# Output stage of a gated mix of a state-space layer and an MLP: when the states are loaded, and where two buffers lie

## The chip, the cores and the metric

The kernel runs on one core of a Trainium2 chip. A core has a matrix engine (TensorE, PE in the profile), three engines for elementwise work (VectorE or DVE, ScalarE or ACT, GpSimd or POOL) and SyncE (SP), which here only issues transfers. Transfers are issued on the queues of SP, ACT and POOL, and 16 DMA engines carry them out. Each engine works through its own queue in order and waits on semaphores for the others.

The metric is the device time of one execution in microseconds, as the median over runs.

## The reference, cut to what matters

The input `x` has 2048 tokens of 1024 features. A gate `g` per token mixes a diagonal complex state-space layer and an MLP with layer norm; everything is given and returned in bfloat16.

```python
def reference(A_x, A_Lambda_re, ..., gate_w):
    def _A_ref(x, ...):
        Lam_bar = jnp.exp(dt * Lam)
        Bu = jnp.einsum("bld,pd->blp", x + 0j, B_bar)
        for t in range(L):
            h = Lam_bar[None, :] * h + Bu[:, t, :]
            hs.append(h)
        hseq = jnp.stack(hs, 1)
        y = 2.0 * jnp.einsum("blp,dp->bld", hseq, Cmat).real + x * Dskip[None, None, :]
        return y
    def _B_ref(x, w1, b1, w2, b2):
        y = _layernorm(x, axis=-1)
        h = _gelu(jnp.einsum("bsd,df->bsf", y, w1) + b1)
        return jnp.einsum("bsf,fd->bsd", h, w2) + b2
    x = A_x
    g = _sigmoid((x * gate_w).sum(-1, keepdims=True))
    a = _A_ref(...)
    b = _B_ref(...)
    return g * a + (1 - g) * b
```

## The kernel before

**Stages.** The kernel first multiplies `x` by `B` and stores the result in device memory, runs the recurrence as scans on DVE beside the MLP's matmuls, and stores the states (`HS`, one tensor of 1 MB for each 256 tokens). The MLP is done in halves of its hidden features: `m` groups compute hidden values into the area HT, `b` groups multiply them by `W2`. What a `b` group yields is scaled by 1 - g (`GM1`) and stored in float32 in `ACS` in device memory; the second half of the features is added there by an accumulating store (`acs1.k` for token tile k of 128 tokens, line 1243, on the POOL queue). Last comes the **output stage**: eight output blocks `y0` to `y7` of 256 tokens, two token tiles each, in the order `YORD` (tokens 1024 to 2047 first), so that `y0` holds token tiles 8 and 9, `y1` 10 and 11, `y4` 0 and 1.

**One group on PE.** Each group of the MLP and each output block is a 2x2 block product in Winograd's form, with seven products in place of eight. They are the phases p1 to p7 of the class `SG`, each 8 (in `b` groups 7) matmuls of 128x128 by 128x512. For block x the order is p1(x), p7(x-1), p5(x), p6(x), p2(x), p3(x), p4(x-1). Around them:

- the sums `ys1` to `ys4` (`y_prep`, made on DVE from the states): ys1 feeds p5, ys2 feeds p6, ys4 feeds p3 and ys3 feeds p7;
- `seed` (line 1053, ACT) copies the bank of p1 into a second bank, on which p6, p7 and p4 go on adding;
- the snapshots `s5` (after p5) and `su` (after p6), written by ACT to the memory on chip (line 1045);
- DVE's `oa` (line 1331, adds a snapshot) and `o` (line 1333, evicts a bank into the output tile), and the store `out` on the ACT queue (line 1338).

**What is loaded** (`y_load`). For block yi: `hg` (line 1298), the states, 1 MB on the SP queue into the slot `H0[yi]`; for each of the two token tiles, ACT's `bb` (line 1307), which fills a float32 slot with the bias; `acl` (line 1309), a load on the POOL queue that adds the MLP's result from `ACS` to that slot; `yx` (line 1310), the tile of `x` on the SP queue; then DVE's `xd` (line 1311, x times D) and `xa` (line 1312, adds it to the slot). `y_load` is called for blocks 0 and 1 at the last `b` group, for 2 and 3 at block 0, and for x+3 at block x.

**Areas.** The memory on chip is one arena with areas laid by hand: HT (the hidden values, 28 KB in each partition), W2Q right behind it (seven quadrants and differences of `W2`, 7 KB each: B11 at 0, B21 at 7168, B22 at 14336, and so on), W1R, XN, SQ, AO (18 KB: four slots of 4 KB for the `b` groups' results on their way to `ACS`, and s5 in the last 2 KB), SSM (20 KB) and TABR. The output stage uses them again. Before the change its eight state slots are two in SSM and six in HT and the first part of W2Q; the sums of even blocks lie in SQ (running 1 KB into AO) and those of odd blocks in AO from 4096 on, `su` of odd blocks in AO from 12288 on. The last two `b` groups' results use slots 0 and 1 (tiles 4 and 5) and 2 and 3 (tiles 6 and 7).

**The order.** The program is a graph of tasks. Dependencies follow from reads and writes of pieces of 256 bytes of the arena, so that a writer waits for all that read the bytes before it. A planner with costs and priorities written into the kernel lays the tasks on the engines' queues once, when the program is built; on the chip each queue keeps that order, whatever the true times are. `hg`, `bb`, `acl`, `yx`, `xd` and `xa` have priority 52, behind all of the MLP's and the output stage's own work (10): the planner fits them in wherever a queue has nothing else ready. `extra` adds dependencies by hand; `pe_last` is a list that holds the task that was last laid on PE.

Of the kernel before, what the change touches and what calls it, by code (L numbers as in the profile page):

```python
# [35 lines left out]
def c_act(N, psum=True, ap_operands=0):  # L36
    return (0.15 if psum else 0.19) + 0.00083 * N + 0.09 * ap_operands


def c_tt16(N):  # L40
    return 0.07 + N / 1920.0


def c_dve(N):
    return 0.09 + N / 960.0
# [374 lines left out]
def build(nc, A_x, A_Lambda_re, A_Lambda_im, A_B_re, A_B_im, A_C_re, A_C_im, A_log_dt, A_Dskip,  # L420
          B_x, B_w1, B_b1, B_w2, B_b2, gate_w, out, stats=None):
# [22 lines left out]
    g = Graph()  # L444
    es = ExitStack()
    with es:
# [5 lines left out]
        def sem(name, dram=False):  # L452
            nsem[0] += 1
            return SemC(es.enter_context(nc.semaphore(name)), name, dram)
# [3 lines left out]
        HS = nc.dram_tensor("scr_h", (L // T, 128, 2 * PT * T), BF16, kind="Internal").ap()  # L458
# [18 lines left out]
        HT = AR.alloc(28672)  # L477
# [3 lines left out]
        SQ = AR.alloc(14336)  # L481
        AO = AR.alloc(18432)
        SSM = AR.alloc(20480)
# [20 lines left out]
        def bc(name):  # L504
            if name not in b_cst:
                b_cst[name] = B("cst." + name)
            return b_cst[name]
# [14 lines left out]
        def ssem(name, k, final=False):  # L522
            key = (name, k)
            if key not in slot_sems:
                slot_sems[key] = sem("d_%s%d" % (name, k), dram=final)
                if final:
                    final_sems.append(slot_sems[key])
            return slot_sems[key]
# [39 lines left out]
        def C(name, j=0, n=1):  # L568
            return V(CST, col[name] + j, [(1, n)])
# [19 lines left out]
        def bcast(ap, off, name):  # L589
# [11 lines left out]
              reads=[b_ones], writes=[b_ident], name="ident")  # L601
# [77 lines left out]
        for k in range(4):  # L679
# [5 lines left out]
              reads=[b_stg, b_ident], writes=[b_ps[bk0]], name="cst_T", extra=[g.tasks[-2]])  # L685
        stage_names = ["LRE", "LIM", "LDT", "DSK", "B2", "GW", "B1"]
        cst_cp = g.add("dve", 0.15, P0, lambda e: e.tensor_copy(V(CST, 0, [(1, NROW)]), V(PS16[bk0], 0, [(1, NROW)])),
              reads=[b_ps[bk0]], writes=[bc(n) for n in stage_names] + [b_ps[bk0]], name="cst_copy")
# [97 lines left out]
        for p0 in range(0, PT, 4):  # L786
# [4 lines left out]
                  reads=[e1i], writes=[vt], name="tab_s%d" % p0)  # L791
        for pt in range(PT):
# [7 lines left out]
                  reads=[pi, bc("E20I")], writes=[td0], name="e2t0_%d" % pt)  # L800
            g.add("dve", 0.3, PT2, lambda e, td1=td1, pr=pr, pt=pt: e.tensor_scalar(td1.ap, pr.ap, C("E20I", pt), None, ALU.mult),
                  reads=[pr, bc("E20I")], writes=[td1], name="e2t1_%d" % pt)
            g.add("dve", c_dve(T), PT2, lambda e, td0=td0, pr=pr, pt=pt, o2=o2: e.scalar_tensor_tensor(o2.ap, pr.ap, C("E20R", pt), td0.ap, ALU.mult, ALU.add),
                  reads=[pr, td0, bc("E20R")], writes=[o2], name="e2r_%d" % pt)
            g.add("dve", c_dve(T), PT2, lambda e, td1=td1, pi=pi, pt=pt, o3=o3: e.scalar_tensor_tensor(o3.ap, pi.ap, C("E20R", pt), td1.ap, ALU.mult, ALU.subtract),
                  reads=[pi, td1, bc("E20R")], writes=[o3], name="ne2i_%d" % pt)
# [3 lines left out]
        b_hs = [[B("hs%d_%d" % (p, h)) for h in range(L // T)] for p in range(PT // 4)]  # L810
# [107 lines left out]
        for pt in range(4, PT):  # L918
            for ri, ap in enumerate((A_B_re, A_B_im)):
                o = AR.v(RB + (pt * 2 + ri) * 2048, [(128, DT), (1, 128)])  # L920
# [6 lines left out]
        for half in range(2):  # L927
            for pt in range(4, PT):
# [4 lines left out]
              reads=[bc(z) for z in zs], writes=[bc("TZ")], name="tanh")  # L933
        g.add("dve", 0.1, (5.0, 0), lambda e: e.tensor_scalar(C("G", 0, NTT), C("TZ", 0, NTT), 0.5, 0.5, ALU.mult, ALU.add),
              reads=[bc("TZ")], writes=[bc("G")], name="G")
        g.add("dve", 0.1, (5.0, 0), lambda e: e.tensor_scalar(C("GM1", 0, NTT), C("TZ", 0, NTT), -0.5, 0.5, ALU.mult, ALU.add),
              reads=[bc("TZ")], writes=[bc("GM1")], name="GM1")
# [6 lines left out]
        PG = PT // 4  # L944
        NQ = L // T
        UE = 8 * T
# [68 lines left out]
        pe_last = []  # L1015
# [230 lines left out]
        nxt_ss = {}  # L1246


        H0 = [SSM + 8192 * i for i in range(2)] + [HT + 8192 * i for i in range(6)]
        YR = HT + 49152  # L1250
        AV = [TABR + 4096 * i for i in range(4)] + [YR + 4096 * i for i in range(4)]
        XV = [SSM + 16384, YR + 16384, YR + 18432]
        DB = SSM + 18432
        OV = [YR + 20480 + 2048 * i for i in range(4)]
        YS = [SQ + 7168, AO + 4096]
        YU = [SSM + 16384, AO + 12288]
        CQ = {"B11": 0, "B21": 1, "B22": 2, "T1": 3, "T2": 4, "T3": 5, "T4": 6, "B12": 6}
        YORD = (4, 5, 6, 7, 0, 1, 2, 3)

        def cq(nm, k=None, dt=None):  # L1260
            dt = dt or (FP16 if nm[0] == "T" else BF16)
            if k is None:
                return AR.v(W1R + CQ[nm] * 8192, [(1, 4096)], dt)
            return AR.v(W1R + CQ[nm] * 8192 + k * 1024, [(1, 512)], dt)
# [9 lines left out]
        def hk(yi, ri, t, k=None):  # L1274
            o = H0[yi] + (ri * T + t * 128) * 2
            if k is None:
                return AR.v(o, [(2 * T, PT), (1, 128)])
            return AR.v(o + k * 4 * T, [(1, 128)])

        def ysq(yi, i, k=None):  # L1280
            o = YS[yi % 2] + i * 2048
            if k is None:
                return AR.v(o, [(128, PT), (1, 128)], FP16)
            return AR.v(o + k * 256, [(1, 128)], FP16)
# [9 lines left out]
        def y_load(yi):  # L1294

            qb = YORD[yi]
            o = AR.v(H0[yi], [(1, 2 * UE)])
            g.dma((52.0, yi), lambda e: e.dma_start(out=o.ap, in_=HS[qb]), 2 * UE * 128 * 2, ssem("hg", yi), reads=[b_hs[pg][qb] for pg in range(PG)], writes=[o], name="hg%d" % yi)
            if yi == 0:
                g.dma((51.0, 0), lambda e: e.dma_start(out=v_db.ap, in_=bass.AP(A_Dskip.tensor, A_Dskip.offset, [[0, 128], [1, D]])), 128 * D * 2, sem("d_dskb"), writes=[v_db], name="dskb")  # L1300
            for t in range(2):
                n = 2 * yi + t
                k = 2 * qb + t
                av = AR.v(AV[n % 8], [(1, D)], F32)
                xi = 0 if n < 4 else 1 + n % 2
                xv = AR.v(XV[xi], [(1, D)])
                g.add("act", c_act(D, psum=False, ap_operands=1), (52.0, n), lambda e, av=av, k=k: e.activation(av.ap, v_b2.ap, AF.Copy, scale=C("GM1", k)),  # L1307
                      reads=[v_b2, bc("GM1")], writes=[av], name="bb%d" % k)
                g.dma((52.0, n), lambda e, av=av, k=k: e.dma_start(out=av.ap, in_=ACS[k], accum_op=ALU.add), 128 * D * 4, ssem("yac", n % 8), reads=[b_acs[k], av], writes=[av], name="acl%d" % k, q="pool").slack = 1.0  # L1309
                g.dma((52.0, n), lambda e, xv=xv, k=k: e.dma_start(out=xv.ap, in_=x2[k * 128:(k + 1) * 128, :]), 128 * D * 2, ssem("yx", xi), writes=[xv], name="yx%d" % k)  # L1310
                g.add("dve", c_tt16(D), (52.0, n), lambda e, xv=xv: e.tensor_tensor(xv.ap, xv.ap, v_db.ap, ALU.mult), reads=[xv, v_db], writes=[xv], name="xd%d" % k)
                g.add("dve", c_dve(D), (52.0, n, 1), lambda e, xv=xv, av=av, k=k: e.scalar_tensor_tensor(av.ap, xv.ap, C("G", k), av.ap, ALU.mult, ALU.add),
                      reads=[xv, av, bc("G")], writes=[av], name="xa%d" % k)

        def y_group(yi):
# [4 lines left out]
            mv = {nm: [cq(nm, k) for k in range(PT)] for nm in ("B11", "B21", "B22", "T1", "T2", "T3", "T4")}  # L1320
            su, s5 = AR.v(YU[yi % 2], [(1, 512)], F32), AR.v(AO + 16384, [(1, 512)], F32)
            done = {}
# [59 lines left out]
        for n, it in enumerate(flat):  # L1382
# [4 lines left out]
            if (kind, Fh, c, x) == ("b", 1, 0, 3):  # L1387
                y_load(0)
                y_load(1)
            if (kind, x) == ("y", 0):  # L1390
                for yi in range(2, 4):
                    y_load(yi)
# [72 lines left out]
def bass_gated_mix__ssm_conv_s5__mixer_channel_mlp__prompt_kernel(  # L1465
    nc, A_x, A_Lambda_re, A_Lambda_im, A_B_re, A_B_im, A_C_re, A_C_im, A_log_dt, A_Dskip,
    B_x, B_w1, B_b1, B_w2, B_b2, gate_w, out,
):
    build(nc, A_x, A_Lambda_re, A_Lambda_im, A_B_re, A_B_im, A_C_re, A_C_im, A_log_dt, A_Dskip,
          B_x, B_w1, B_b1, B_w2, B_b2, gate_w, out)  # L1470
# [28 lines left out]
```

## Time and profile before

| what | value |
|---|---|
| time, median of 6 runs | 584.19 us (582.49 to 585.09) |
| time of the profiled execution | 584.37 us |
| its span, first to last instruction | 582.6 us |
| mean granted clock of TensorE | 0.994 |
| PE busy / DVE busy / ACT busy / POOL busy | 96% / 82% / 47% / 13% |
| DMA | 134.76 MB, mean 231 GB/s |
| state loads `hg` after 440 us | 6 of 1024 KB, median 15.2 us from issue to landing |
| accumulating loads `acl` after 440 us | 12 of 512 KB, median 8.7 us |
| stores `acs` after 440 us | 7 of 512 KB, median 11.6 us |
| `x` tiles `yx` after 440 us | 13 of 256 KB, median 4.8 us |

The span is what the profiler sees between the first and the last instruction; the time of the same execution is 1.8 us longer. Busy shares are averages over stages with different limits, so they say only which engine can't have much room over the whole span. The granted clock is 1 where TensorE runs at full speed. The last four rows are from the output stage and its entry: between issue and landing a transfer may stand behind others in its queue, and shares the 16 DMA engines with the other queues.

### The profile page before, as it was taken

How to read it: one execution, taken by the hardware profiler on the slowest of the kernel's cores; microseconds unless marked ns; L12 is line 12 of the kernel's file. 1: busy time of each engine (PE TensorE's matmuls, PEld its weight loads, DVE VectorE, ACT ScalarE, POOL GpSimd, SP SyncE). 2: the span in 40 equal slices, each digit the busy share in tenths (PEclk: the TensorE clock that was granted, in tenths of full speed). 3: DMA queues.
4: the chain of work that ended last, by engine and by line, in shares of the span. 5: the costliest groups of instructions: out<-in, count | busy, mean ns of one | idle time of the engine just before them, and what ended most of it. 6: DMA issues, size and time to landing. Idle time of an engine off the chain costs nothing.

```text
span 582.6 us, 7345 instructions
## 1 busy us (share of the span) xinstructions
PE 557.2 (96%) x2608; PEld 254.1 (44%) x2657; DVE 479.0 (82%) x817; ACT 272.3 (47%) x433; POOL 75.3 (13%) x110
## 2 busy tenths in 40 slices
PE   5999999998999999999999999999999996899997
PEld 4544444443444444444444444444444442344442
DVE  3897749959999999999999999996457745699843
ACT  3935861456773236862346763248652431222210
POOL 0070161000100110011110102221001130111000
PEclk9999999999999999999999999999999997999999
DMA  8999949998599354667398799896998699897411
GB/s 273 262 259 371 354 92 316 251 334 326 177 335 287 112 217 173 203 217 283 130 335 292 241 273 268 152 189 230 298 262 153 134 287 300 239 211 180 126 52 54
DMA packets 124543, 134.76 MB, mean 231 GB/s; under 512 B 70482, under 2 KB 100178, under 8 KB 123482
## 3 DMA queue, kind: packets, MB, share of 16 engines
q1 hardware_dynamic: 99664, 70.81, 43.4%
q0 software_dynamic: 11232, 46.40, 28.9%
q10 hardware_dynamic: 13610, 17.08, 8.8%
q8 instruction: 21, 0.34, 0.2%
q14 instruction: 16, 0.13, 0.1%
HBM read 63.74 MB, written 54.80 MB: 203 GB/s over the span
## 4 chain that ended last, share of the span: by engine, by line
PE 72%; DVE 15%; DMA 7%; issue 3%; ACT 1%; SPq 1%; ACTq 0%; DVEq 0%; POOLq 0%
PE ps L1029 44%; PE ps L1027 16%; PE ps L825 11%; DMA scr_ac<-ar 5%; DVE ar L970 3%; DVE ar L984 3%; DVE ar L1081 3%; DVE ar L973 2%; DVE ar L1163 2%; DMA ar<-in_B_w_dram 2%; DVE ar L871 1%; DMA ar<-in_A_x_dram 1%; PE ps L666 1%; PE ps L650 0%; DVE ar L1333 0%
## 5 line engine op out<-in xcount | busy, mean ns | idle before, releaser
L1029 PE MATMUL ps<-ar 128*128 128x512 f16 (+1 forms) x1419 | 326.7, 380 | 6.9 <-ACT ar L1045 3.8
L1029 PEld LDWEIGHTS ps<-ar 128*128 128x128 f16 (+1 forms) x1440 | 140.7, 98 | 178.3 <-ACT ar L1045 4.7
L1027 PE MATMUL ps<-ar 128*128 128x512 f16 (+1 forms) x560 | 139.2, 383 | 7.5 <-DVE ar L1081 6.8
L1081 DVE TENSOR_TENSOR ar<-ar 128x896 f16<-128x896 bf16 (+8 forms) x176 | 118.6, 709 | 28.8 <-DMA scr_ac<-ar 9.7
L825 PE MATMUL ps<-ar 128*128 128x512 bf16 x500 | 110.4, 379 | 0.7 <-issue 0.2
L1027 PEld LDWEIGHTS ps<-ar 128*128 128x128 bf16 (+1 forms) x576 | 56.3, 98 | 76.9 <-DVE ar L1081 9.2
L984 DVE TENSOR_TENSOR_SCAN ar<-cst,init,ar 128x256 bf16<-128x256 f32 x128 | 86.9, 731 | 0.3
L970 DVE TENSOR_TENSOR ar<-ar 128x2048 bf16<-128x2048 bf16 x64 | 77.0, 1217 | 3.0 <-DMA ar<-scr_u 2.9
L825 PEld LDWEIGHTS ps<-ar 128*128 128x128 bf16 x512 | 49.7, 98 | 59.6 <-issue 0.4
L1045 ACT ACTIVATE ar<-ps 128x512 f32<-128x512 f32 x72 | 42.3, 593 | 47.2 <-PE ps L1027 28.5
L832 ACT ACTIVATE ar<-ps 128x512 bf16<-128x512 f32 x64 | 37.1, 596 | 48.1 <-PE ps L825 25.4
L1163 DVE TENSOR_TENSOR ar<-ps,ar 128x512 f32<-128x512 f32 x56 | 38.1, 680 | 11.7 <-PE ps L1029 11.5
L1165 ACT ACTIVATE ar<-ar,cst 128x512 bf16<-128x512 f32 x56 | 40.3, 720 | 14.7 <-DVE ar L1163 14.4
L1046 ACT ACTIVATE ar<-ps,cst 128x512 f32<-128x512 f32 x32 | 22.1, 689 | 53.4 <-PE ps L1027 33.7
L1159 ACT ACTIVATE ar<-ps,cst 128x512 bf16<-128x512 f32 x56 | 38.3, 687 | 17.9 <-PE ps L1029 17.5
L1053 ACT ACTIVATE ps<-ps 128x512 f32<-128x512 f32 x52 | 30.3, 583 | 33.7 <-PE ps L1027 26.7
L973 DVE TENSOR_TENSOR ar<-ar 128x1024 bf16<-128x1024 bf16 x64 | 42.0, 685 | 0.3
L1231 ACT ACTIVATE ar<-ps,cst 128x512 f32<-128x512 f32 x32 | 22.1, 689 | 41.7 <-PE ps L1029 41.7
L1333 DVE SCALAR_TENSOR_TENSOR ar<-ps,cst,ar 128x512 bf16<-128x512 f32 x32 | 23.8, 747 | 13.9 <-PE ps L1029 13.9
L1307 ACT ACTIVATE ar<-ar,cst 128x1024 f32<-128x1024 bf16 x16 | 18.3, 1146 | 28.7 <-DVE ar L1333 27.1
L1234 DVE SCALAR_TENSOR_TENSOR ar<-ps,cst,ar 128x512 f32<-128x512 f32 x32 | 23.7, 739 | 6.5 <-PE ps L1029 6.3
L1309 POOL DMA_DIRECT2D ar<-scr_ac x16 | 14.0, 878 | 93.2 <-ACT ar L1307 55.0
(98 smaller groups left out, 224.0 us busy)
## 6 DMA issues: line engine op xcount, KB each, us to landing
scr_ac<-ar POOLq DMA_DIRECT2D x32, 512.0 KB, 5.5
scr_w<-ar POOLq DMA_DIRECT2D x14, 896.0 KB, 6.1
ar<-scr_w SPq DMA_DIRECT2D x14, 896.0 KB, 6.3
ar<-in_A_x_dram SPq DMA_DIRECT2D x32, 256.0 KB, 4.9
scr_u<-ar ACTq DMA_DIRECT2D x32, 256.0 KB, 5.7
ar<-scr_u SPq DMA_DIRECT2D x16, 512.0 KB, 8.0
scr_h<-ar POOLq DMA_DIRECT2D x16, 512.0 KB, 5.7
ar<-scr_ac POOLq DMA_DIRECT2D x16, 512.0 KB, 8.7
```

What stands on the lines that cost most here:

```text
L825: ins = e.matmul(V(PS[bk], 0, [(1, CH)]), ws[dt].ap, xs[dt].ap, start=(dt == 0), stop=(dt == DT - 1))
L832: g.add("act", c_act(CH), pr, lambda e, ev=ev, bk=bk: e.activation(ev.ap, V(PS[bk], 0, [(T, 2), (1, T)]), AF.Copy), reads=[b_ps[bk]], writ ...
L970: g.add("dve", c_tt16(UE), pri(i), lambda e: e.tensor_tensor(o.ap, a.ap, tbl.ap, ALU.mult), reads=[a, tbl], writes=[o], name=nm + tag)
L973: g.add("dve", c_tt16(UE // 2), pri(i), lambda e: e.tensor_tensor(o.ap, a.ap, b.ap, op), reads=[a, b], writes=[o], name=nm + tag)
L984: lambda e, pt=pt, ri=ri, vin=vin, go=go: e.tensor_tensor_scan(go.ap, Cb("R", pt, T), vin.ap, V(INIT, pt * 2 + ri, [(1, 1)]), ALU.mult, AL ...
L1027: ins = e.matmul(V(PS[bk], 0, [(1, n)]), st[i].ap, mv[i].ap, start=(i == 0), stop=(i == K - 1))
L1029: ins = e.matmul(V(PS[bk], 0, [(1, n)]), st[i].ap, mv[i].ap, start=False, stop=(i == K - 1), skip_group_check=True)
L1045: return e.activation(o.ap, V(PS[bk], 0, [(1, 512)]), AF.Copy)
L1081: g.add("dve", c_tt16(n), (10.0, q), lambda e: e.tensor_tensor(o.ap, a.ap, b.ap, op), reads=[a, b], writes=[o], name=nm).slack = slack
L1159: g.add("act", c_act(512, ap_operands=1), (10.0, q + 1), lambda e: e.activation(o.ap, V(PS[bk], 0, [(1, 512)]), AF.Gelu_apprx_tanh, bias=C ...
L1163: g.add("dve", c_dve(512), (10.0, q - 2), lambda e: e.tensor_tensor(sv.ap, V(PS[bk], 0, [(1, 512)]), sv.ap, ALU.add), reads=[b_ps[bk], sv] ...
L1165: g.add("act", c_act(512, psum=False, ap_operands=1), (10.0, q + 3), lambda e: e.activation(o.ap, sv.ap, AF.Gelu_apprx_tanh, bias=C("B1", ...
```

## The change

The state slots become a ring of six: blocks 6 and 7 use the two slots in SSM again, after blocks 0 and 1. The sums of odd blocks (`YS[1]`) move from AO to the place that the slot of block 6 had, in the quadrants B11 and B21 of W2Q, and `su` of odd blocks (`YU[1]`) to the start of the former slot of block 7, in B21. The state loads of blocks 4 to 7 get a dependency on the task that was last laid on PE when `y_load` is called for them, which is p4 of the block x-1 where the call is made at block x: p4 of blocks 0, 1, 2 and 3 for the loads of blocks 4, 5, 6 and 7.

```diff
-        H0 = [SSM + 8192 * i for i in range(2)] + [HT + 8192 * i for i in range(6)]
+        H0 = [SSM, SSM + 8192] + [HT + 8192 * i for i in range(4)] + [SSM, SSM + 8192]
         YR = HT + 49152
...
-        YS = [SQ + 7168, AO + 4096]
-        YU = [SSM + 16384, AO + 12288]
+        YS = [SQ + 7168, HT + 32768]
+        YU = [SSM + 16384, HT + 40960]
...
-            g.dma((52.0, yi), lambda e: e.dma_start(out=o.ap, in_=HS[qb]), 2 * UE * 128 * 2, ssem("hg", yi), reads=[b_hs[pg][qb] for pg in range(PG)], writes=[o], name="hg%d" % yi)
+            g.dma((52.0, yi), lambda e: e.dma_start(out=o.ap, in_=HS[qb]), 2 * UE * 128 * 2, ssem("hg", yi), reads=[b_hs[pg][qb] for pg in range(PG)], writes=[o], name="hg%d" % yi,
+                  extra=pe_last if yi > 3 else ())
```

The planner lays the queues anew. In the built program PE's order is the same. On DVE the sums of block 1 stand earlier, among the last `b` group's work; `xa13`, `xa12`, `xa15` and the following `xd` and `xa` take other places among the evictions, and `xa12` stands ahead of `o9.1`. On ACT, `seed` of block 1 comes before its neighbour `bb0`, and `seed` of block 2 comes after `out9` and `bb1`, where it stood before `out9`. On SP the state loads are spread: behind load 3 come `yx15`, `yx14`, `yx1`, load 4, `yx0`, load 5, `yx2`, `yx3`, load 6, `yx4`, `yx5`, load 7, `yx6`, `yx7`; before, loads 2, 6 and 7 stood together, and 3, 4 and 5. POOL's order is the same.

## Prediction

> **What bounds the kernel now.** I read the page first. TensorE (PE) is busy 96% of the span and makes up 72% of the chain that ended last, so only time in which PE stands still, or runs slowly, can be won. In the chain one link is no engine at all:
>
> ```profile
> PE 72%; DVE 15%; DMA 7%; issue 3%; ACT 1%; SPq 1%; ACTq 0%; DVEq 0%; POOLq 0%
> PE ps L1029 44%; PE ps L1027 16%; PE ps L825 11%; DMA scr_ac<-ar 5%; DVE ar L970 3%; DVE ar L984 3%; DVE ar L1081 3%; DVE ar L973 2%; DVE ar L1163 2%; DMA ar<-in_B_w_dram 2%; DVE ar L871 1%; DMA ar<-in_A_x_dram 1%; PE ps L666 1%; PE ps L650 0%; DVE ar L1333 0%
> ```
>
> Second, the chain in order of time (start, length, what) says where that link lies: at the entry to the output stage, one store of the MLP result takes 26.87 us, and behind it PE runs without a break until the last phase.
>
> ```profile
> 475.66 26.87 DMA scr_ac<-ar
> 507.33 7.08 PE ps L1029 x32
> 514.46 1.67 PE ps L1027 x7
> 516.14 1.73 PE ps L1029 x8
> ```
>
> Third, the waits of PE from 230 us to the end (total, times, longest). All but the 0.8 (the tail, which stays) and 0.8 of the 5.9 lie in 480 to 508 us:
>
> ```profile
> PE ps L1027 <- DVE ar L1081: 5.9, 3, 5.1
> PE ps L1029 <- ACT ar L1045: 1.8, 1, 1.8
> PE ps L1029 <- DVE ar L1333: 0.8, 1, 0.8
> PE ps L1029 <- ACT ps L1053: 0.5, 1, 0.5
> ```
>
> Fourth, the timeline of that stretch (start, length, then idle time and what ended it). The sums of output block 1 on VectorE (DVE) wait for the stores of the MLP staging they are written over: first ys3_1, then, at 487.36, ys1_1, which PE waits for. Then ScalarE (ACT) can't write the snapshot su_1 before the last store lands, and PE waits again:
>
> ```profile
> 483.67 0.69 DVE L1081 TENSOR_TENSOR ar<-ar 128x1024 f16<-128x1024 bf16 x1 [5.08 <-DMA scr_ac<-ar]
> ...
> 487.36 1.42 DVE L1081 TENSOR_TENSOR ar<-ar 128x1024 f16<-128x1024 bf16 x2 [1.14 <-DMA scr_ac<-ar]
> ...
> 488.11 3.60 PE L1027 MATMUL ps<-ar 128*128 128x512 f16 x8 [5.13 <-DVE ar L1081]
> ...
> 491.50 8.15 PE L1029 MATMUL ps<-ar 128*128 128x512 f16 x32
> ...
> 502.56 0.60 ACT L1045 ACTIVATE ar<-ps 128x512 f32<-128x512 f32 x1 [10.16 <-DMA scr_ac<-ar]
> ...
> 503.21 1.90 PE L1029 MATMUL ps<-ar 128*128 128x512 f16 x8 [1.84 <-ACT ar L1045]
> ```
>
> Fifth, three stretches of it (start:end, length, busy time of PE, PE's weight loads, DVE, ACT, POOL; the last three numbers are the granted clock, the DMA share and GB/s). After the 5.1 us pause the clock is at half, and the DMA engines are full:
>
> ```profile
> 483.00:486.00 3.00, 0.00 (x0) 0.00 (x0) 2.33 (x4) 0.54 (x1) 0.00 (x0) 1.00 1.05 274
> 486.00:488.00 2.00, 0.00 (x0) 0.00 (x0) 0.86 (x2) 1.09 (x2) 0.86 (x1) 0.71 1.06 326
> 488.00:490.00 2.00, 1.89 (x5) 0.73 (x6) 1.97 (x5) 0.00 (x0) 0.00 (x0) 0.50 1.06 311
> ```
>
> **What the waits cost.** Idle: 5.13 + 1.84 + 0.49 = 7.5 us. Slow clock: 8 matmuls from 488.11 to 491.50 took 3.39 against 1.73 in the chain, and the next 32, to 499.70, took 8.20 against 6.91: 1.66 + 1.29 = 2.95. Together 10.4. Check: from block 0's first phase (469.43) to 507.33 PE has 127 matmuls of 0.216 (6.91 / 32), 27.4 us; it took 37.9, so 10.5 were lost.
>
> **Part 1, the buffers.** YS[1] (the sums of odd blocks) and YU[1] (their su) leave AO for the area of W2's quadrants B11 and B21. Their new owners are PE's phases p1 and p2 of the last MLP group; p2 ends at about 464.8 (five phases fill 461.66 to 469.4). In the built program ys1_1, ys3_1 and ys2_1 stand behind DVE's work that ended at 464.4, 0.6 each, before the eviction of p3 (466.42 now, 467.2 at most then; its bank is wanted at 483.0). So both waits for stores go: 10.4 us. ys4_0 still overlaps AO's first KB and waits for the store acs1.4 (landed 470.6), but is due at 477.6. Nothing is added on PE, whose order is the same.
>
> **Part 2, the state loads.** Loads 4 to 7 (1 MB each) now wait for the last phase (p4) of blocks 0 to 3, and 6 and 7 reuse SSM. This takes 4.2 MB out of 465 to 502 us. It matters through the queues: loads 6 and 7 were issued at 464.9 and 466.4, and the x tiles 12 and 13 behind them on SP landed only at 482.9 and 486.1. Meanwhile the Pool queue's transfers (512 KB each) landed at 470.6, 475.7, 480.5, 483.6, 487.3, 492.9 (accumulating load acl12), 498.0, 502.5: 3.2 to 5.5 apart, where two stores with nothing beside them landed 2.96 apart.
>
> What is late next? The new DVE order has xa12 (adds x·D to the loaded sum; needs acl12) **ahead of** the eviction o9.1 and all that follows, so acl12 decides. Six Pool transfers follow the one that lands at 467.3. At 2.96 each: 485.0; at today's pace: 492.9. With only load 3 and two x tiles beside them I take 3.15 each, the gap seen beside x tiles alone (480.5 to 483.6): 486. From there, by the spacing in the timeline (1.2 an xa, 0.66 an eviction or oa, 0.6 a sum or xd): xa12 to 487.2; then thirteen instructions to o9.0, one xa, six evictions or oa, six sums or xd, 1.2 + 4.0 + 3.6 = 8.8: 496.0. ACT holds the seed of block 2 behind the issue of out9 (0.36) and bb1 (1.15): with its own 0.58 and hand-overs, 498.3. PE, unhindered from 483.0 at 1.73 a phase, wants it for block 2's p6 at 496.8. **New wait: 1.5 us**, 0 if acl12 lands by 484.5, one more for each us later; over 3.4 it would bear on the clock.
>
> There a rule counts. The trace shows half clock after a 5.1 us pause (falling between 486 and 488) and none after 1.84. The Trainium skill (TensorE: Matmul & The Clock Gate, Part 1) puts the fall at about 3.4 us of idling. By the rows alone a pause of 3 to 4 is open; by the rule it would add up to 2.95. At 1.5 neither adds anything.
>
> The loads themselves: p4 of block 0 ends at 491.6. Load 4 stands on SP behind yx1, which waits for xa15 (the tenth instruction after xa12, done at 494); behind it wait yx0, then loads 5 to 7 with two x tiles each, which feed xd and xa. Load 4, issued at 494, lands after 6 (load 1 took 5.9) to 10 us (load 6 beside others: 9.7): 500 to 504. DVE reaches its sums at about 503 (behind o12.0, which needs block 2's p2, 501.8); PE wants them near 520, but o11.0 behind them releases out11, bb3 and the seed of block 3 (508.9, wanted 510.4): the cover is 1.5 us. Load 5: p4 of block 1, about 505, lands by 511 to 515, its sums come up some 12 us after load 4's, at 515 to 518. Loads 6 and 7 repeat this 12.1 us apart. Cost 0 to 2. The Trainium skill (DMA: Bandwidth & Descriptors, Rules for kernel authors) speaks against this part: issue a transfer early and wait late. By it a load issued so late shows what it takes beyond its cover, 0 to 2 us at each of four; by the rows the early issue is what stretched them (loads 3 to 5 took 16.9, 22.0 and 26.5) and the stores with them. I follow the rows, and add 0.5 us for the 12 us periods that now carry a load, two accumulating loads, two x tiles and two outputs (3.1 MB).
>
> **Sum.** 584.37 (span 582.6 and 1.8 around it) - 10.4 + 1.5 + 0.5 = 576.0. The median shown, 584.19, is 0.2 below the profiled execution, inside the spread; I keep 576.0.
>
> **Rivals.**
> 1. *All of it, no new wait* (acl12 by 484.5): 584.4 - 10.4 = 574.0. For: Pool alone could be there at 485. Against: load 3 falls into it. 15%.
> 2. *The accumulating load is slow by itself*: acl12 lands at 492.9 as now. o9.1 then ends at 494.9 and p4 of block 0 waits 5.0; the clock falls, 2.95; the seed wait shrinks to 0.5. 574.0 + 8.4 = 582.4. Against: its pace followed what ran beside it. 8%.
> 3. *Loads 4 to 7 late by 1 to 1.5 us each*: about 579. 6%.
> 4. *Slower: the DMA engines become the bound of blocks 2 to 5.* From 490 to 545 they would have to move 13.9 MB (4 state loads, 8 accumulating loads and a store, 9 x tiles, about 10 outputs): 253 GB/s. For it: today 510 to 520 shows a DMA share of 0.93 at only 209 GB/s, as if 225 were the limit; then 62 us, 6.8 lost. It eats the whole gain below 219 GB/s; at 210 the stretch takes 66 us, and the time is 584.4 - 10.4 + 1.5 + 11 = 586.5. Against: 485 to 500 moved 315 to 324 with the same kinds of transfer, so the share is packets that wait, not the limit. 10%.
> 5. *It does not do what it says*, another wait sits at the same spot: 584. For: ys4_0's leftover overlap. Against: its store lands 7 us early. 3%.
>
> The forecast has the remaining 58%. Range: 573.3 (rival 1 less the spread) to 581.5 (rival 3, and acl12 up to 491). About 0.2%, 1.2 us, is what a measurement can tell from no change. Faster 0.85, same 0.05, slower 0.10.
>
> **What would show it.** Right: no DVE or ACT wait for scr_ac stores after 472 us; block 1's p5 on PE at 483 with the clock at 1.00 throughout; x tiles 12 and 13 landed before 477; acl12 at 485 to 488; a PE wait below 3 us for ACT's L1053 near 497; state loads of 6 to 9 us; DVE still ahead of PE in blocks 4 to 7. Wrong: PE waits for L1081 behind a state load, periods over 12.1 us in blocks 3 to 6 (rival 4), or DVE held for an accumulating load past 490 (rival 2).

## The result, and the profile after

The changed kernel takes 580.24 us (median of 31 runs, 575.18 to 585.98) against 585.1 for the kernel before, run beside it (median of 68, 581.68 to 593.97): ratio 0.9906, 95% interval 0.9889 to 0.9923. That is 5.5 us less (4.5 to 6.5), where 8.2 were forecast; the time lies inside the range. Ratios here and below compare the fast executions alone, without those more than 1.5% above the fastest of their kernel, so they differ a little from the ratio of the medians.

Its profiled execution has a span of 579.7 us. It entered the output stage (block 0's first phase on PE) at 470.93, 1.5 us later than the execution of before did (469.43), but the change did not make that difference: it is there already at PE's short wait near 262 us (261.5 before, 262.9 after). Over the profiled executions of this study the entry lies between 468.2 and 472.7. So two profiles are best compared by the **stage**, from that phase to the end: 113.2 us before, 108.8 after. PE's arithmetic with the tail, as the prediction adds it up, needs 113.2 - 10.4 = 102.8.

The dependency adds one line to the kernel, so in every run that has it the lines behind 1298 have numbers higher by one than those given above: `xd` is 1312, `xa` 1313, `o` 1334.

PE's waits after the change, from 230 us to the end (total, times, longest):

```profile
PE ps L1029 <- ACT ps L1053: 4.2, 2, 3.8
PE ps L1029 <- DVE ar L1334: 0.9, 1, 0.9
PE ps L1027 <- DVE ar L1081: 0.8, 2, 0.5
```

The waits of 5.1 and 1.8 us have gone, and no engine waits for a store of the MLP result any more. What is left is the tail (0.9), 0.8 us long before the stage, and a new wait, for ACT's line 1053, the seed. The chain in order of time tells what stands behind it (start, length, what; pieces under 0.9 us are left out):

```profile
470.99 17.01 DMA ar<-scr_ac
488.02 1.30 DVE ar L1313
489.34 7.41 DMA ar<-in_A_x_dram
497.38 1.28 DVE ar L1313
499.75 1.15 ACT ar L1308
501.12 0.93 issue
502.68 8.77 PE ps L1029 x32
511.50 1.67 PE ps L1027 x7
```

Read from the top: the accumulating load acl12 lands at 488.0; xa12 uses it and so frees its x tile's slot; only then can x tile 14 be sent, and it takes 7.4 us; xa15 stands behind that on DVE; then come the evictions, the outputs and the bias bb1 on ACT, and the seed. The 32 matmuls after it take 8.77 us in place of 6.91. The timeline of the same stretch shows each engine's idle time and what ended it:

```profile
482.75 0.69 DVE L1312 TENSOR_TENSOR ar<-ar 128x1024 bf16<-128x1024 bf16 x1 [2.30 <-DMA ar<-in_A_x_dram]
...
486.61 7.08 PE L1029 MATMUL ps<-ar 128*128 128x512 f16 x32 [0.41 <-ACT ps L1053]
...
488.02 1.28 DVE L1313 SCALAR_TENSOR_TENSOR ar<-ar,cst 128x1024 f32<-128x1024 bf16 x1 [1.94 <-DMA ar<-scr_ac]
...
496.77 0.69 DVE L1312 TENSOR_TENSOR ar<-ar 128x1024 bf16<-128x1024 bf16 x1 [2.41 <-DMA ar<-in_A_x_dram]
...
502.68 8.77 PE L1029 MATMUL ps<-ar 128*128 128x512 f16 x32 [3.81 <-ACT ps L1053]
```

Three stretches of it (start:end, length, busy time of PE, PE's weight loads, DVE, ACT, POOL; then granted clock, DMA share, GB/s):

```profile
496.00:498.00 2.00, 2.00 (x11) 0.89 (x10) 1.23 (x2) 0.00 (x0) 0.00 (x0) 1.00 0.10 21
498.00:500.00 2.00, 0.87 (x5) 0.20 (x2) 2.00 (x4) 0.25 (x1) 0.00 (x0) 1.00 0.01 3
...
504.00:506.00 2.00, 2.00 (x6) 0.72 (x5) 0.59 (x2) 0.60 (x1) 0.00 (x0) 0.50 0.98 335
```

The DMA engines stand idle from 496.8 to nearly 500, just when DVE has run late for want of an x tile: the next tiles and load 4 all wait, one behind the other on SP's queue, for instructions of DVE, and Pool's next load (issued at 501.2) waits for the bias bb2, which stands on ACT behind out10, and so for DVE too. Then PE pauses, and the clock falls to half.

The account: pauses 3.81 + 0.41, slow clock 8.77 - 6.91 = 1.86, together 6.1; 102.8 + 6.1 = 108.9, where 108.8 was measured.

### The profile page after: what moved, and what is told of

It is laid out like the page before. It is cut to its first block, busy times and chain, and to the rows that moved or that the text cites. A ratio compares the mean times of both kernels' runs of the same rounds, so it can differ in the third digit from the quotient of the medians.

```text
span 579.7 us, 7338 instructions
## 1 busy us (share of the span) xinstructions
PE 556.0 (96%) x2608; PEld 253.7 (44%) x2657; DVE 479.2 (83%) x817; ACT 272.1 (47%) x433; POOL 76.5 (13%) x110
## 4 chain that ended last, share of the span: by engine, by line
PE 71%; DVE 16%; DMA 7%; issue 3%; SPq 1%; ACT 1%; ACTq 0%; POOL 0%; DVEq 0%
PE ps L1029 44%; PE ps L1027 16%; PE ps L825 11%; DVE ar L984 3%; DMA ar<-scr_ac 3%; DVE ar L1081 3%; DVE ar L970 3%; DMA ar<-in_A_x_dram 2%; DVE ar L973 2%; DVE ar L1163 2%; DMA ar<-in_B_w_dram 2%; DVE ar L871 1%; PE ps L666 1%; DVE ar L1313 0%; DVE ar L1334 0%
## 5 line engine op out<-in xcount | busy, mean ns | idle before, releaser
L1159 ACT ACTIVATE ar<-ps,cst 128x512 bf16<-128x512 f32 x56 | 38.3, 687 | 17.9 <-PE ps L1029 17.4
```

Of the source, the lines that this page charges most:

```text
L1159: g.add("act", c_act(512, ap_operands=1), (10.0, q + 1), lambda e: e.activation(o.ap, V(PS[bk], 0, [(1, 512)]), AF.Gelu_apprx_tanh, bias=C ...
```

## The experiments

All ratios are to the kernel before on the same chip, with 95% intervals. "Stage" and "PE waits" are from one profiled execution each. The waits leave out the tail's 0.9. In e1_buffers and e2_defer the planner laid the queues anew, so that orders changed along with the edit; the other runs hold the orders of the kernel that they start from, but for what they move by hand.

| run | loads 4 to 7 wait for PE | buffers moved | other | ratio | stage, us | PE waits in the stage, us |
|---|---|---|---|---|---|---|
| before | no | no | | 1 | 113.2 | 5.1, 1.8, 0.5 |
| the change | yes | yes | | 0.9906 (0.9889 to 0.9923) | 108.8 | 3.8, 0.4 |
| e1_buffers | no | yes | | 0.9939 (0.9913 to 0.9965) | 110.3 | 4.4, 0.2 |
| e2_defer | yes | no | | 0.9886 (0.9837 to 0.9934) | 105.9 | 1.5, 1.3 |
| e3_xslot | yes | yes | own slot for x tile 14 | 0.9884 (0.9821 to 0.9946) | 106.2 | 2.9 |
| e4_seed | yes | yes | seed of block 2 ahead | 0.9896 (0.9848 to 0.9944) | 108.6 | 3.0, 0.5, 0.3 |
| f1_seeds | yes | yes | seeds 2 to 7 ahead | 0.9844 (0.9794 to 0.9893) | 104.7 | 0.9, 0.6 |
| f2_ring5 | yes | yes | five x slots | 0.9875 (0.9827 to 0.9924) | 106.2 | 3.1, 0.2 |
| f3_ring5_seeds | yes | yes | both of these | 0.9811 (0.9773 to 0.9849) | 102.8 | none |
| f4_defer_seeds | yes | no | seeds 1 to 7 ahead | 0.9794 (0.9758 to 0.9829) | 102.7 | none |
| g1_seeds_only | no | no | seeds 1 to 7 ahead | 0.9996 (0.9954 to 1.0037) | 114.2 | 5.1, 2.2 |
| g2_buffers_seeds | no | yes | seeds 1 to 7 ahead | 0.9923 (0.9884 to 0.9962) | 109.3 | 5.1 |

### The two halves of the change

**e1_buffers**: the changed kernel without the dependency.

```diff
-            g.dma((52.0, yi), ..., name="hg%d" % yi,
-                  extra=pe_last if yi > 3 else ())
+            g.dma((52.0, yi), ..., name="hg%d" % yi)
```

> The changed kernel without the dependency of the state loads 4 to 7 on PE: buffers and ring of six alone. Loads 4 and 5 are then issued at once behind load 3, 6 and 7 as soon as blocks 0 and 1 have been read. My theory (the transfers in flight set when the accumulating load acl12 lands, and DVE's queue stands behind it): no wait for stores on block 1's sums or su, but acl12 lands 3 to 5 us later than in the changed kernel, about 491 us, so that p4 of block 0 waits 1 to 4 us and the seed of block 2 another 3 to 4, with the clock falling: 1 to 5 us slower than the changed kernel, ratio to before 0.993 to 0.999. Rival (the late loads do nothing, the buffers are the whole change): the same as the changed kernel, 0.990.

The ratio lies in the theory's range and above the rival's 0.990, though its interval still touches that of the changed kernel (0.9889 to 0.9923); and the way it came about is not the one expected. acl12 landed at 487.85, 18.2 us after the entry against 17.1 in the changed kernel: 1.2 later, not 3 to 5. Loads 4 and 5 stood on SP's queue behind load 3, which landed at 486.5, and landed after acl12, at 491.9 and 497.3. What was late were the x tiles. The chain, and the wait of PE that it ends in:

```profile
469.83 18.03 DMA ar<-scr_ac
487.88 1.30 DVE ar L1312
489.19 15.40 DMA ar<-in_A_x_dram
505.57 1.04 issue
507.41 3.60 PE ps L1029 x8
```

x tile 14 takes 15.4 us and tile 15 takes 17.2, because loads 3, 4 and 5 stand ahead of them on SP's queue. DVE waits 5.2 us for one and 1.9 for the other, PE 4.4 for the eviction behind them, and then runs at half clock (8 matmuls in 3.60). The ring of six is part of this run: load 6 could be sent only at 492.4 and load 7 at 511.0, so half of the deferral is still in it.

**e2_defer**: the dependency on the kernel before, and nothing else.

```diff
-            g.dma((52.0, yi), ..., name="hg%d" % yi)
+            g.dma((52.0, yi), ..., name="hg%d" % yi,
+                  extra=pe_last if yi > 3 else ())
```

> The kernel before with nothing but the dependency of the state loads 4 to 7 on p4 of blocks 0 to 3; all buffers as before. My theory: with 4 MB out of the way the stores of the MLP staging land some 5 to 10 us earlier (the last at about 493 to 495), so that block 1's first sum is held 0 to 1 us past its due time and su of block 1 hardly; the seed of block 1 may wait 1 to 2 us, that of block 2 0 to 3: 5 to 8 us faster than before, ratio 0.986 to 0.992, as good as or better than the whole change. Rival (the shared buffers are what costs, whatever is in flight): the waits for stores stay at 5 and 1.8 us, ratio 0.997 to 1.000.

Its waits of PE:

```profile
PE ps L1029 <- ACT ps L1053: 2.8, 2, 1.5
PE ps L1029 <- DVE ar L1334: 0.9, 1, 0.9
```

As the theory had it. The buffers are still shared, and DVE (5.6 us in all) and ACT (5.9) still wait for the stores, but the stores land early enough (the store that ys1_1 waits for, acs1.5, 12.7 us after the entry, against 17.9 before; the last store 23.2 against 33.1) that PE does not: the 5.1 and the 1.8 are gone without the buffers being moved. By ratio this half is as good as the whole change.

### Where the new wait comes from

**e3_xslot**: one more slot for x tile 14; queue orders written out by hand so that they stay those of the changed kernel (the lists are left out here).

```diff
-        XV = [SSM + 16384, YR + 16384, YR + 18432]
+        XV = [SSM + 16384, YR + 16384, YR + 18432, HT + 43008]
...
-                xi = 0 if n < 4 else 1 + n % 2
+                xi = 0 if n < 4 else 3 if n == 6 else 1 + n % 2
```

> The changed kernel with one more slot for an x tile, used by token tile 14 alone, so that its load no longer waits for xa12; the order on every queue is held as in the changed kernel. My theory (xd14 on DVE waited 2.4 us for that tile, and pushed the seed of block 2 past the point at which the clock falls): the wait of xd14 goes, the pause of PE before block 2's p6 falls from 3.8 to 1.0 to 2.0 us, the clock stays at full: 3 to 5 us faster than the changed kernel, ratio to before 0.982 to 0.986. Rival (the transfer only moves the contention, acl12 and acl15 land later by as much): 0 to 1 us, ratio 0.989 to 0.991.

The timeline, DVE's wait for that tile and PE's for the seed:

```profile
495.05 0.69 DVE L1312 TENSOR_TENSOR ar<-ar 128x1024 bf16<-128x1024 bf16 x1 [1.24 <-DMA ar<-in_A_x_dram]
...
500.97 7.08 PE L1029 MATMUL ps<-ar 128*128 128x512 f16 x32 [2.94 <-ACT ps L1053]
```

Between the two. The tile was sent at 484.4, behind load 3 and tile 15 on SP, and landed at 495.0: half of its wait went (1.24 for 2.41), and so did the slow clock (32 matmuls in 7.08; the last section shows that this hung on where the pause fell), while acl12 came only 0.2 later. The pause only fell to 2.9. The interval of the ratio holds both theories' values.

**e4_seed**: one instruction moved on ACT's queue, after the planner is done.

```diff
         g.schedule(horizon=HORIZON)
+        od = g.order["act"]
+        mt = next(t for t in od if t.name == "seed_y2")
+        od.remove(mt)
+        od.insert(next(i for i, t in enumerate(od) if t.name == "out10"), mt)
```

> The changed kernel with one instruction moved on ACT's queue: the seed of block 2 stands before out10, bb2, out9 and bb1 instead of behind them. My theory (PE's pause of 3.8 us and the slow clock after it come from this place in the queue): PE has no pause before block 2's p6, the clock stays at full; the snapshot s5 of block 2, still behind bb1, may hold p3 of block 2 for up to 1 us: 4.5 to 6 us faster than the changed kernel, ratio to before 0.980 to 0.983. Rival (PE would wait for DVE's evictions a little later in any case): 0 to 2 us, ratio 0.987 to 0.991.

The rival's size was right, though PE did not wait for an eviction directly. The pause before block 2 went, and came back one block later, at the seed of block 3, which stands behind out11 and bb3 in the same manner:

```profile
514.52 5.80 PE L1029 MATMUL ps<-ar 128*128 128x512 f16 x19 [3.03 <-ACT ps L1053]
```

There DVE had waited 2.8 us for x tile 0, which was sent behind load 4. So the lateness of DVE and the place of the seeds are two separate things, and the next runs took them one at a time.

**f1_seeds**: all seeds of blocks 2 to 7 ahead.

```diff
         g.schedule(horizon=HORIZON)
+        od = g.order["act"]
+        for yi in range(2, 8):
+            mt = next(t for t in od if t.name == "seed_y%d" % yi)
+            od.remove(mt)
+            od.insert(1 + next(i for i, t in enumerate(od) if t.name == "su_y%d" % (yi - 1)), mt)
```

> The changed kernel with the seeds of blocks 2 to 7 each moved on ACT's queue to directly behind the su of the block before, ahead of the outputs and biases. The run that moved the seed of block 2 alone only pushed the pause to the seed of block 3. My theory (a pause is DVE held by a late x tile, and reaches PE through the outputs that stand ahead of a seed on ACT): with all seeds ahead, the x tiles are as late as before (7 to 10 us), DVE waits for them as before, but PE's waits in blocks 1 to 6 sum to less than 1.5 us and the clock stays at full: from block 0's first phase to the end 103 to 105 us against 108.8 in the changed kernel; ratio to before 0.981 to 0.986. Rival (DVE is so late that PE next waits for an eviction or for a bank, 2 us or more): 106 to 109 us, ratio 0.987 to 0.991.

By the stage, 104.7, the theory's, though the interval of the ratio reaches the rival's 0.987 too. DVE waited 7.8 us in all for x tiles and 4.4 for accumulating loads, as late as ever, but of that only 1.5 us reached PE (the first line holds the tail as well):

```profile
PE ps L1029 <- DVE ar L1334: 1.8, 2, 0.9
PE ps L1029 <- ACT ar L1045: 0.6, 1, 0.6
```

**f2_ring5**: the seeds left where the change has them, the x tiles mended (the written-out orders of DVE and ACT, which are those of the changed kernel, are left out).

```diff
-        XV = [SSM + 16384, YR + 16384, YR + 18432]
+        XV = [SSM + 16384, YR + 16384, YR + 18432] + [HT + 43008 + 2048 * i for i in range(3)]
...
-                xi = 0 if n < 4 else 1 + n % 2
+                xi = 0 if n < 4 else 1 + n % 5
...
+            "sp": ("hg2 yx12 yx13 yx15 hg3 yx14 yx0 yx2 yx1 hg4 yx3 yx4 hg5 yx5 hg6 yx6 yx7 hg7").split(),
```

> The changed kernel with five rotating slots for the x tiles of token tiles 4 to 15 in the order of use, in place of two, and SP's queue laid so that x tiles go out ahead of the state loads where a slot is free; the order of PE, DVE, ACT and POOL is that of the changed kernel. My theory (the two slots make the x tiles late, while the DMA engines stand idle at 498 to 500 us): DVE waits for x tiles no more after block 1, PE's pause at the seed of block 2 is 0.5 to 2.5 us (acl12 alone), the clock stays at full: 103.5 to 105.5 us from block 0's first phase to the end, ratio to before 0.982 to 0.987. Rival (the transfers sent earlier delay acl12 and load 3 by 2 us or more, so that DVE waits there instead): 107 to 110 us, ratio 0.988 to 0.993.

The timeline:

```profile
489.42 1.28 DVE L1313 SCALAR_TENSOR_TENSOR ar<-ar,cst 128x1024 f32<-128x1024 bf16 x1 [6.08 <-DMA ar<-scr_ac]
...
501.58 7.08 PE L1029 MATMUL ps<-ar 128*128 128x512 f16 x32 [3.08 <-ACT ps L1053]
```

DVE waits for no x tile any more, and the stage lies between what the two theories gave. With the tiles that now go out early beside it, acl12 took longer: 18.6 us from issue to landing against 17.0, and DVE waits 6.1 us for it in one piece. Part of the gain went straight into the other wait, as the rival had it, though less than its 2 us.

**f3_ring5_seeds**: both edits.

> Both of the two edits before this together: five slots for x tiles and the seeds of blocks 2 to 7 ahead on ACT's queue. My theory: nothing of the new waits is left but the seed of block 1 (0.5 us, x tile 13) and the tail: 102.7 to 104 us from block 0's first phase to the end, where the arithmetic of PE alone gives 102.8; ratio to before 0.980 to 0.985, no slower than either edit alone. Rival (the edits undo each other, by load 3 or acl12 coming later): 105 us or more.

PE has no wait left in the stage but the tail's, and the stage is the arithmetic's 102.8. DVE still waits 7.7 us for accumulating loads.

### The version that beats both kernels, and what it needs

**f4_defer_seeds**: the kernel before with the dependency alone, and the loop of f1_seeds from block 1 on (`range(1, 8)`).

> The kernel before with the dependency of the state loads on PE alone (all buffers as before) and the seeds of blocks 1 to 7 each moved on ACT's queue to directly behind the su of the block before. My theory (in the run with the dependency alone, PE waited only for two seeds, 1.5 and 1.3 us, and the shared buffers cost nothing once the stores land in time): these go; a wait of under 1 us for block 1's first sum or su may stay: 103 to 104.5 us from block 0's first phase to the end, ratio to before 0.980 to 0.986, as good as the changed kernel with the same edit. Rival (once the seeds are out of the way the shared buffers hold PE after all, by the stores): 106 us or more, ratio 0.988 or above.

All waits of PE from 465 us to the end:

```profile
PE ps L1029 <- DVE ar L1334: 0.9, 1, 0.9
```

573.21 us (median of 6), 2.1% under the kernel before, with no buffer moved. DVE and ACT wait for the shared buffers' stores for 5.3 and 6.1 us, all of it beside PE's work. The mean granted clock of all executions agrees: 0.999 or 1.000 in 17 of the 18 of f1_seeds, f3_ring5_seeds and f4_defer_seeds, in 2 of the 32 of the changed kernel, and in none of the 61 of the kernel before that ran beside these runs.

Two controls show that the seeds need the dependency. **g1_seeds_only** has the loop of f4 on the kernel before:

> The kernel before with nothing but the seeds of blocks 1 to 7 moved ahead on ACT's queue. My theory (before, PE's two long waits were for stores, through the shared buffers; the seed's place cost 0.5 us): DVE's first sum of block 1 still waits for the store and PE for it, 4 to 5 us, su of block 1 another 1.5 to 3, the clock falls: 112 to 114 us from block 0's first phase to the end, ratio 0.996 to 1.000. Rival (the place of the seeds is most of what the last kernel won, and the late loads little): 108 us or less, ratio 0.990 or below.

Nothing is gained without the dependency: PE waits 5.1 us for ys1_1 and 2.2 for su, where it waited 5.1 and 1.8 before. **g2_buffers_seeds** has the moved buffers with the same loop:

> The buffers and the ring of six alone (no dependency of the loads on PE), with the seeds of blocks 1 to 7 moved ahead on ACT's queue. My theory (without the dependency, load 4 and 5 stand on SP's queue ahead of x tiles 15 and 14 and make these 15 to 17 us long; DVE then holds evictions and with them PE's banks, which no place of a seed can mend): PE keeps the wait for DVE's eviction, 3 to 5 us, and the slow clock: 108.5 to 111 us from block 0's first phase to the end, ratio 0.991 to 0.996, more than 1% slower than the dependency with the same edit. Rival (that wait came through the seeds as well): 104 to 106 us, ratio 0.980 to 0.986.

The theory's again: PE waits 5.1 us for the eviction that x tiles 15 and 14 hold up, and the clock falls.

## Why the prediction was right in its sign and too large in its size

**What PE loses before (10.4 us): right.** Both waits for stores went, and the stage of the kernel without new waits (f3_ring5_seeds, f4_defer_seeds) is 102.8 and 102.7, which is 113.2 - 10.4.

**Part 1, the buffers: the wait named was right, the credit was not.** The prediction gave the 10.4 us to the move of the buffers and let the loads matter "through the queues". Each half takes the two waits away from PE by itself, and the dependency alone (0.9886, and 0.9794 with the seeds of blocks 1 to 7) does no worse than with the buffers moved (0.9906, and 0.9844 with those of blocks 2 to 7). Once the loads are held back, no gain of the move could be measured.

**Part 2, the next wait: its place right, its size wrong.** acl12 was put at 486; it landed at 488.0, or 486.5 when the later entry is taken off. The wait was put at the seed of block 2 behind out9 and bb1, and there it was. Its size was put at 1.5 us and was 3.8. The term that failed is in the sum of "thirteen instructions to o9.0 ... 8.8", which took xd14 to be ready: its x tile can be sent only after xa12, and took 7.4 us where the tiles of the stage before had a median of 4.8. DVE waited 2.4 us for it, and 1.5 + 2.4 is the pause: from the landing of acl12 to the end of o9.0 it took 12.5 us where the prediction had 10.0. (acl12 itself was half a microsecond later than forecast, and PE, held at block 1, was 0.4 later too; these two cancel.) e3_xslot, f2_ring5 and e4_seed support this from three sides, but they also show that there is no single culprit: take one late transfer away and the next (tile 13, acl12, tile 0) holds DVE nearly as long. What turned each of them into a pause of PE is the place of the seed on ACT.

**The clock: its price left out of the sum, through the size of the wait.** The text said that a pause over 3.4 us would bear on the clock, and took the pause to be 1.5. It was 3.8, and cost 1.86 more; but the 3.4 was not what decided (last section). A third, small term was missing too: x tile 13 was to land by 477 and landed at 482.7, which delayed out8 and with it the seed of block 1, for which PE waited 0.4. With the three terms in place the sum is 10.4 - 3.8 - 1.9 - 0.4 = 4.3, the 4.4 of the two stages. The profiled execution of the change took 581.5, more than its median of 580.2, so the loss in a usual execution is somewhat smaller, as the 5.5 us of the ratio say. That the time lies inside the range is in part luck: its upper end was set for late state loads and for acl12 up to 491, neither of which came, and not for an x tile that stalls DVE.

**The late loads: right.** Loads 4 to 7 took 6.6, 5.8, 6.2 and 6.9 us, load 4 sent at 499.1 instead of 494, because yx1 ahead of it on SP waited for xa15, to which DVE came late; and no wait of PE in blocks 4 to 7 stands behind one. The 0.5 us set aside for fuller periods was not needed. What they may have cost is hidden in the x tiles behind them on the same queue, which took 7 to 10 us in blocks 2 to 5. The rule of the Trainium skill (DMA: Bandwidth & Descriptors, Rules for kernel authors) to issue early, which spoke against this part, was outweighed by the rows: e2_defer, which does nothing but issue later, is 6.7 us faster than before (3.9 to 9.6 by its interval).

**The rivals.** The DMA engines as the bound (rival 4) did not come: from 520 to 540 they moved 268 and 269 GB/s, above the 219 below which it would have eaten the whole gain, and PE's periods there are 12.1 us. acl12 as late as before (rival 2) did not come either, nor in e1_buffers, where half of the loads were still sent early.

## What to carry to other kernels

A buffer that is shared with a slow store can be mended at the other end: here holding back transfers that nobody needed yet did as much as moving the buffer, with one line. On an engine whose queue is fixed when the program is built, follow the chain across queues: a late transfer stalls DVE, an output on ACT waits for DVE, and the one instruction that PE needs stands behind that output; moving it ahead cost nothing that the traces show, and with the loads held back it took more from the stage (to 104.7 us) than speeding up the x tiles did (106.2), one trace each and with intervals of the ratio that overlap. Without the loads held back it won nothing (g1_seeds_only, g2_buffers_seeds). When adding up such a chain, ask of every instruction in it when its own operand can first be sent, and not only of the first.

## What the runs showed of the hardware that was not expected

The clock does not fall at one fixed length of pause. With full clock before it, a pause of PE of 1.84 us (before), 2.94 (e3_xslot) and 3.08 (f2_ring5) left it at full, but 3.03 (e4_seed), 3.81 (the change), 4.42 (e1_buffers) and 5.13 (before) were followed by half clock, and so was one of only 2.17 us, in the run with the seeds alone:

```profile
504.00 3.57 PE L1029 MATMUL ps<-ar 128*128 128x512 f16 x8 [2.17 <-ACT ar L1045]
```

The traces show what decides. In each of them all changes of the clock lie whole multiples of 3.41 us apart (in the change the rise at 507.40 and the fall at 579.08, behind the last matmul, 21 times), so that they mark a grid, whose place differs from run to run; a stretch of half clock in mid-run lasts 3.41 us (the change, e4_seed) or 6.83 (before, e1_buffers). Here are PE's busy time and the clock in windows cut along that grid (columns as above): two windows of the change and the one after them, then two of e3_xslot, then one of g1_seeds_only and the one after it:

```profile
497.16:500.57 3.41, 1.71 (x8) 0.59 (x6) 3.41 (x6) 0.82 (x1) 0.00 (x0) 1.00 0.15 56
500.57:503.99 3.42, 1.31 (x7) 0.60 (x7) 3.42 (x6) 2.48 (x4) 1.70 (x2) 1.00 1.07 289
503.99:507.40 3.41, 3.41 (x10) 1.17 (x9) 1.05 (x2) 0.60 (x1) 0.00 (x0) 0.50 0.99 297
...
496.44:499.86 3.42, 1.59 (x8) 0.50 (x6) 3.42 (x5) 1.73 (x2) 0.38 (x1) 1.00 0.60 137
499.86:503.27 3.41, 2.30 (x11) 1.09 (x12) 2.72 (x5) 1.93 (x4) 1.32 (x2) 1.00 0.89 314
...
500.60:504.02 3.42, 1.25 (x7) 0.40 (x6) 0.04 (x1) 0.67 (x2) 0.00 (x0) 1.00 1.06 255
504.02:507.43 3.41, 3.41 (x9) 1.20 (x10) 3.23 (x5) 1.42 (x2) 0.00 (x0) 0.50 0.69 203
```

The pause of the change leaves 1.7 us idle in the first window and 2.1 in the second, and the clock falls at the end of the second; that of e3_xslot is split into 1.8 and 1.1 and costs nothing; the 2.17 of g1_seeds_only lie in one window and are enough. So it is in all twelve traces: at full clock, every window with 2.1 us or more of idle PE was followed by half clock, and none with 1.9 or less. A window at half clock costs about half of its 3.4 us (1.86 in the change). The Trainium skill (TensorE: Matmul & The Clock Gate, Part 1) has a free-running window of about 3.4 us, which these traces show, and lets the clock fall after an idle one; here a window that was idle for 2.1 us counted. A pause can be split between two windows, so by these numbers (an estimate) one of up to 1.9 us is free, one of over 4.2 is not, and between them it hangs on where the pause falls.

A transfer's time from issue to landing depends on what stands ahead of it on its own queue: x tiles of 256 KB took 2.6 us with nothing ahead of them (yx1 in the change), 7.4 behind another tile and with Pool's transfers beside them (tile 14), and 15 to 17 in e1_buffers behind two or three state loads of 1 MB. It depends on the other queues too: the accumulating load acl12, with the same transfers ahead of it on Pool's queue, took 23.4 us before, where loads 6 and 7 landed in its time as well, and 17.0 after the change.
